# Gated linear attention with two expert layers: chunks prepared two ahead, then three, with other first loads and constant matrices built on the chip

## The chip, the cores and the metric

The kernel runs on one core of a Trainium2 chip. The metric is the time of one launch on the device, in microseconds (us), as the median of several runs. The engines of a core are named as the profile names them: PE (TensorE, matrix products; PEld are its weight loads), DVE (VectorE), ACT (ScalarE), POOL (GpSimd) and SP (SyncE, which here only issues DMAs). Each engine executes its own queue in order; semaphores hold an instruction until what it needs is done.

## The reference

Three layers follow each other. The first is the attention below, over 4 batches, 8 heads, 768 steps and a head width of 48. The second sends each token whose skip score is above zero to the expert with the largest gate logit (8 experts, 384 to 1024 to 384, relu), scales by the gate's probability and adds the token; the third takes the maximum of three products and multiplies by an output matrix.

```python
for t in range(S):
    state = alpha[:, :, t, :, None] * state + np.einsum('bhd,bhe->bhde', k[:, :, t], v[:, :, t])
    y[:, :, t] = np.einsum('bhd,bhde->bhe', q[:, :, t], state)
```

## The kernel before, in words

The sequence of each batch is cut into 6 chunks of 128 steps; 4 batches make 24 chunks, counted n = 0 to 23, and two heads share the 128 partitions, so that a chunk is 4 head pairs wide. The attention takes about the first 135 us; the expert layers, which stay as they are, take the rest. All instructions stand in the order in which the Python code emits them (`manual_schedule`): nothing reorders them afterwards.

For a chunk j, the coefficients, k and q come in one tile `akq` (772.5 KiB: 260.5 of coefficients, 256 each of k and q), of which there are four buffers. `load(j)` fetches all of it, `load_part(j, i)` the coefficients (i = 0), k (1) or q (2), `vload(j)` the values `vt` (200 KiB). All go through SP's one queue. `prep(j)` is made of three parts:

- `suffixes` (L224): a scan on DVE gives the products towards the chunk's end, `sf` (L229); ACT keeps the totals; POOL makes the scaled keys `k` (L232).
- `inverse` (L235): a reciprocal on DVE (L237).
- `prefixes` (L239): a second scan on DVE gives `ap` (L243); ACT does a range test; POOL makes the scaled queries `q` (L247); and `load(j + 4)` is issued on SP into the buffer that j has used up.

The loop over n (L491) then does, in this order: `scores(n+1)` on PE (products `ps`, L272), `trans(n+1)` on PE (transposed keys `pk`, L263), one or two preparations, `mask(n+1)` on DVE in two halves (`sm`, L278; the next scores write into the same two PSUM tiles, so they wait for these), `rows(n-1)` (products `px` on PE, L318, with the constant `rps`; a reduction on DVE, L326), `outs(n)` (products `py` on PE, L305 and L308) and `upd(n)` (products `pu` on PE, L290, to which DVE adds the old state, L293; not for the last chunk of a batch). Which chunks are prepared is `pre` (L492): chunk 2 in turn 0, chunks 3 and 4 in turn 1, and chunk n + 3 in each turn from 2 on. `warm(6)` in turn 1 issues six matmuls on PE whose result nobody reads; `warm(15)` does the same at the start.

`patterns` (L465) is called in turn 3. It fills three small tiles `rst` on POOL and copies them on DVE into `pcs`, which the routing of tokens uses from turn 7 on. In turns 3 to 6, SP also issues 16 writes of a tile of zeros (`zt`) over the DRAM buffer `slots`; the scatters that follow each batch's routing (POOL, L418, `slots<-xr`) go into it and wait for these writes.

Of the kernel before, what the change touches and what calls it, by code (L numbers as in the profile page):

```python
# [9 lines left out]
F32 = mybir.dt.float32  # L10
# [10 lines left out]
NP = H // 2  # L21
# [30 lines left out]
XP = 4  # L52
IX = 6
FIRST = (0, 6, 2)
KEEP = (0, 6)
GT = 512
SOFF = 8192.0 + CAP * NE
LAG = 2
# [23 lines left out]


@with_exitstack
def tile_gla_moe_moe2(ctx, tc, akq, vp, rp, wgt, cst, io, ew, md, out):
    nc = tc.nc
    V, A, G, T, SY = nc.vector, nc.scalar, nc.gpsimd, nc.tensor, nc.sync

# [36 lines left out]
        (eng or V).tensor_tensor(l, src, h.bitcast(F32), ALU.subtract)  # L125

    with tc.manual_schedule():
        cs = const.tile([128, 3 * 128 + NTILE + 8], F32, name="cs")
        rps = const.tile([PR, NP, 105], F32, name="rps")
        ident = cs[:, 0:128]  # L130
        cmask = cs[:, 128:256]
        tokid = cs[:, 384:384 + NTILE]
        rev = cs[:, 384 + NTILE:]
        ltri = const.tile([128, 128], BF16, name="ltri")
        ones = const.tile([128, 128], BF16, name="ones")
        low = const.tile([PR, 1], F32, name="low")
# [48 lines left out]
        zt = w1p.tile([128, XW], F32, name="zt")  # L185
        zero = w1p.tile([128, 1], F32, name="zero")
        ws = [w1p.tile([PR, NP * D + 16], F32, name=f"ws{i}") for i in range(2)]

        def warm(n):
            pw = ps_r.tile([128, 512], F32, name="pr")  # L190
# [16 lines left out]
        def load_part(j, i):  # L207
            raw_[j] = lds[j % LDB]
            z = (slice(0, KW), slice(KW, KW + NP * C), slice(KW + NP * C, AQ))[i]
            SY.dma_start(out=raw_[j][:, z], in_=akq[seq[j]][:, z])  # L210

        def vload(j):
            if j >= nseq:
                return
            b, c = seq[j]
            vt[j] = hp.tile([128, VW], F32, name="vt")
            SY.dma_start(out=vt[j], in_=vp[b, :, c])
# [17 lines left out]
        def inverse(j, sf):  # L235

            V.reciprocal(raw_[j][:, pads], sf[:, pads])  # L237
# [203 lines left out]
            split(h, l, rw[s // 4][:, s % 4 * EW:(s % 4 + 1) * EW], eng)  # L441
            wr[s] = h, l

        for j, i in ((0, 0), (0, 1), (1, 0), (0, 2)):
            load_part(j, i)
        SY.dma_start(out=cs, in_=cst)
        for i in (1, 2):
            load_part(1, i)
        vload(0)
        load(2)  # L450
        SY.dma_start(out=rps, in_=rp)
        vload(1)
        load(3)
        for j in range(2, 5):
            vload(j)
        prep(0)
        for t in ws:
            G.memset(t[:, NP * D:], 0.0)
        G.memset(cnt, 0.0)
        G.memset(zero, 0.0)  # L460
        G.memset(zt, 0.0)
        G.memset(zt[:, DM + 1:], float(1 << 20))
        A.copy(ltri, cs[:, 256:384])
        def patterns():
            for n in (NC, 4, 2):  # L465
                t = w1p.tile([128, NE * (n + 1)], BF16, name=f"rst{n}")
                G.memset(t, 1.0)
                G.memset(t[:, ::n + 1], 0.0)
                V.tensor_scalar(cols[n].bitcast(I32), t.bitcast(I32), 0, None, ALU.bitwise_or)
            V.tensor_copy(cols["rev"], rev)  # L470
# [17 lines left out]
        scores(0)  # L488
        trans(0)
        prep(1)  # L490
        mask(0, 0)  # L491
        mask(0, 1)  # L492
        for n, (b, c) in enumerate(seq):
            pre = [n + 2] if n == 0 else [n + 2, n + 3] if n == 1 else [n + 3]
            pre = [j for j in pre if j < nseq]
            if n + 1 < nseq:
                scores(n + 1)
                trans(n + 1)
            for j in pre:
                prep(j)  # L500
            if n + 1 < nseq:
                mask(n + 1, 0)
                mask(n + 1, 1)
            low_part = rows(n - 1) if n else None
            outs(n)
            upd(n)
            if n > nseq - 4:
                low_part()
            vload(n + 5)
            if n and seq[n - 1][1] == NC - 1:  # L510
                routes.append(route(b - 1, 0, NC))
            step_routes()
            if n < 2:
                warm(KEEP[n])
            if n == 3:
                patterns()
            if n == 10:
                SY.dma_start(out=iota, in_=io)
            if 3 <= n < 7:
                for i in range((n - 3) * NSLOT // 512, (n - 2) * NSLOT // 512):  # L520
                    SY.dma_start(out=slots[i * 128:(i + 1) * 128, :], in_=zt)
            if 7 <= n < 11:
                wpart(n - 7)
# [865 lines left out]
```

## Time and profile before

| | us |
|---|---|
| median of 3 runs | 579.27 |
| lowest and highest | 579.08, 579.62 |
| the profiled execution, whole | 578.67 |
| its span, first to last instruction | 576.9 |
| PE busy in the span | 561.8 (97%) |
| DVE, ACT, POOL busy | 413.9, 299.9, 255.2 |

Times in the rows count from the start of the span. A row of the timeline says when a group of instructions began, how long it lasted, on which engine and line, what it wrote and read, and in square brackets how long the engine had been idle before and what ended that. A matmul of 32-bit data shows as two records. The granted clock of PE is 1.00 throughout.

### The profile page before, as it was taken

To read this page: it belongs to the slowest core of one execution; us is meant where nothing else is said; L and a number is where in the kernel's file an instruction comes from. 1 tells how busy PE (TensorE), PEld (TensorE's weight loads), DVE (VectorE), ACT (ScalarE), POOL (GpSimd) and SP (SyncE) were. 2 spreads that over 40 slices of the span, in tenths; PEclk is the share of its full clock that TensorE was granted. 3 is DMA by queue.
4 is the path that set the end of the run, shared out by engine and by line. 5 is a ranking of instruction groups with operands and counts; after the bars stand their busy time and mean duration, and the time that the engine had idled before them with its cause. 6 is when DMAs were issued, how large, how long until landed. Compare 5 with 4: busy or idle time off the path is not lost. (4 is left out here: it accounts for less than half of the span.)

```text
span 576.9 us, 11055 instructions
## 1 busy us (share of the span) xinstructions
PE 561.8 (97%) x4155; PEld 500.7 (87%) x4155; DVE 413.9 (72%) x727; ACT 299.9 (52%) x641; POOL 255.2 (44%) x202
## 2 busy tenths in 40 slices
PE   7999999999999999999999999999999999999997
PEld 4789888888899999999988888888887899887897
DVE  7988998967577767777679897593767674675710
ACT  3556675654566766666334445454454474445320
POOL 5554598752456555665222122122464400446320
PEclk9999999999999999999999999999999999999999
DMA  8979998925669888885519139515664633556011
GB/s 312 349 236 341 304 326 314 336 116 193 212 217 332 300 302 294 272 306 214 170 27 295 46 121 380 182 55 203 207 241 144 210 119 109 220 177 233 3 55 61
DMA packets 51008, 123.06 MB, mean 213 GB/s; under 512 B 4579, under 2 KB 38865, under 8 KB 47361
## 3 DMA queue, kind: packets, MB, share of 16 engines
q1 hardware_dynamic: 47712, 116.45, 58.4%
q0 software_dynamic: 2560, 4.83, 2.2%
q10 hardware_dynamic: 672, 0.98, 0.6%
q8 instruction: 34, 0.56, 0.4%
q14 instruction: 30, 0.24, 0.1%
HBM read 93.03 MB, written 32.28 MB: 217 GB/s over the span
## 5 line engine op out<-in xcount | busy, mean ns | idle before, releaser
L125 POOL TENSOR_TENSOR wl<-raw,wh 128x768 fp32r<-128x768 f32 x26 | 53.4, 2054 | 32.4 <-ACT wh L124 32.4
L124 ACT CAST wh<-raw 128x768 fp32r<-128x768 f32 x64 | 53.5, 835 | 16.4 <-PE po L696 15.7
L676 PE MATMUL ph<-xh,wh 128*128 128x256 f32 x192 | 56.4, 294 | 0.0
L677 PE MATMUL ph<-xl,wh 128*128 128x256 f32 x192 | 54.5, 284 | 0.1
L678 PE MATMUL ph<-xh,wl 128*128 128x256 f32 x192 | 54.4, 283 | 0.0
L694 PE MATMUL po<-wh,hh 128*128 128x384 f32 x128 | 43.5, 340 | 0.0
L696 PE MATMUL po<-wh,hl 128*128 128x384 f32 x128 | 43.3, 338 | 0.0
L695 PE MATMUL po<-wl,hh 128*128 128x384 f32 x128 | 43.2, 337 | 0.0
L125 DVE TENSOR_TENSOR wl<-raw,wh 128x768 fp32r<-128x768 f32 x38 | 36.2, 953 | 9.2 <-ACT wh L124 9.2
L682 DVE SCALAR_TENSOR_TENSOR hl<-ph,hh 128x256 fp32r<-128x256 f32 x64 | 26.8, 419 | 16.6 <-ACT hh L681 16.5
L232 POOL TENSOR_TENSOR k<-akq,sf 128x512 f32<-128x512 f32 x24 | 28.5, 1187 | 22.0 <-DVE sf L229 16.2
L418 POOL DMA_INDIRECT slots<-xr,si x24 | 24.8, 1034 | 28.0 <-DVE xr L415 11.8
L677 PEld LDWEIGHTS ph<-xl,wh 128*128 128x128 f32 x192 | 36.5, 190 | 0.5 <-DVE xl L125 0.5
L676 PEld LDWEIGHTS ph<-xh,wh 128*128 128x128 f32 x192 | 36.6, 191 | 0.2 <-ACT xh L124 0.2
L678 PEld LDWEIGHTS ph<-xh,wl 128*128 128x128 f32 x192 | 36.4, 190 | 0.0
L272 PE MATMUL ps<-q,k 64*128 64x128 f32 x384 | 30.2, 286 | 6.3 <-POOL q L247 4.4
L272 PEld LDWEIGHTS ps<-q,k 64*128 64x128 f32 x384 | 24.8, 187 | 10.4 <-POOL q L247 5.8
L681 ACT ACTIVATE hh<-ph 128x256 fp32r<-128x256 f32 x64 | 24.5, 383 | 14.3 <-PE ph L678 13.0
L243 DVE TENSOR_TENSOR_SCAN ap<-akq,pcs 128x521 f32<-128x521 f32 x24 | 29.8, 1241 | 2.2
L229 DVE TENSOR_TENSOR_SCAN sf<-akq,pcs 128x520 f32<-128x520 f32 x24 | 29.4, 1226 | 2.4 <-DMA akq<-in_akq_dram 1.5
L278 DVE TENSOR_TENSOR sm<-ps,cs 128x512 f32<-128x512 f32 x48 | 30.3, 674 | 0.9 <-PE ps L272 0.9
L247 POOL TENSOR_TENSOR q<-akq,ap 128x512 f32<-128x512 f32 x24 | 28.4, 1183 | 5.1 <-DVE ap L243 2.6
(655 smaller groups left out, 1720.9 us busy)
## 6 DMA issues: line engine op xcount, KB each, us to landing
raw<-in_ew_dram SPq DMA_DIRECT2D x15, 1536.0 KB, 7.1
akq<-in_akq_dram SPq DMA_DIRECT2D x22, 772.5 KB, 6.0
rm<-in_md_dram SPq DMA_DIRECT2D x12, 768.0 KB, 6.2
mh<-wd SPq DMA_DIRECT2D x7, 1024.0 KB, 5.0
ml<-wd SPq DMA_DIRECT2D x7, 896.0 KB, 6.6
raw<-wd SPq DMA_DIRECT2D x6, 1024.0 KB, 5.1
raw<-wd SPq DMA_DIRECT2D x6, 896.0 KB, 6.5
vt<-in_vp_dram SPq DMA_DIRECT2D x24, 200.0 KB, 6.3
```

Of the source, the lines that this page charges most:

```text
L124: A.copy(h, src)
L125: (eng or V).tensor_tensor(l, src, h.bitcast(F32), ALU.subtract)
L229: V.tensor_tensor_scan(sf[:, KW - 2::-1], al[:, KW - 1:0:-1], eb[:, KW - 1:0:-1], 0.0, ALU.mult, ALU.max)
L243: V.tensor_tensor_scan(ap, al, eb, 0.0, ALU.mult, ALU.max)
L272: T.matmul(ps[i][:, p, :], kh[j][r0:r0 + 64, p, :], qh[j][r0:r0 + 64, p, :], start=True, stop=True)
L278: V.tensor_tensor(t, fr[j][i], cmask[:, None, :].to_broadcast([128, NP, C]), ALU.mult)
L676: T.matmul(ph, wh[:, z], xh_[e][:, k, :], start=(k == 0), stop=False)
L677: T.matmul(ph, wh[:, z], xl_[e][:, k, :], start=False, stop=False)
L678: T.matmul(ph, wl[:, z], xh_[e][:, k, :], start=False, stop=(k == k3 - 1))
L694: T.matmul(po, hh[:, zm], wh, start=(f == 0), stop=False)
L695: T.matmul(po, hh[:, zm], wl, start=False, stop=False)
L696: T.matmul(po, hl[:, zm], wh, start=False, stop=(f == nf1 - 1))
```

## The change

The order of the first loads changes: all three parts of chunk 0 come first, then the coefficients of chunk 1, the constants, the rest of chunk 1, and chunk 2 in three parts. `vload(3)` and `vload(4)` are issued later. The input `rp` (210 KiB) is gone; ACT builds `rps` from the unit matrix and from 36 columns that are now part of `cst`, which is 162 KiB instead of 208 because it no longer carries the matrix for `ltri`. POOL makes `ltri` as a difference of two matrices, in `patterns`.

Turn 0 prepares chunk 2, turn 1 chunk 3, turn 2 chunk 4. From there the lead grows by one in halves: at the end of turns 2, 3 and 4, `first_half` does `suffixes` and `inverse` of chunks 5, 6 and 7, and the following turn does their `prefixes`. From turn 5 on, `prep(n + 3)` is back. The six matmuls of `warm(6)` are gone. The filling of `ws` moves ahead of all loads, that of `cnt` and `zero` into `patterns`, that of `zt` into turn 2.

```diff
-        for j, i in ((0, 0), (0, 1), (1, 0), (0, 2)):
+        for j, i in ((0, 0), (0, 1), (0, 2), (1, 0)):
             load_part(j, i)
         SY.dma_start(out=cs, in_=cst)
+        for j, i in ((1, 1), (1, 2), (2, 0)):
+            load_part(j, i)
+        vload(0)
         for i in (1, 2):
-            load_part(1, i)
-        vload(0)
-        load(2)
-        SY.dma_start(out=rps, in_=rp)
+            load_part(2, i)
         vload(1)
         load(3)
-        for j in range(2, 5):
-            vload(j)
+        vload(2)
         prep(0)
...
         def patterns():
+            G.memset(cnt, 0.0)
+            G.memset(zero, 0.0)
+            G.tensor_tensor(ltri, cmask, ident, ALU.subtract)
             for n in (NC, 4, 2):
...
         prep(1)
+        vload(3)
+        A.copy(rps[:, :, 0:96].rearrange("p a (i d) -> p a i d", i=2),
+               ident.rearrange("p (i d) -> p i d", i=2)[:, None, :, 0:D].to_broadcast([128, NP, 2, D]))
+        A.copy(rps[:, :, 96:], cs[:, 288:].rearrange("p (a e) -> p a e", a=NP))
         mask(0, 0)
         mask(0, 1)
+        ahead = {}
+
+        def first_half(j, n):
+
+            sf = suffixes(j)
+            inverse(j, sf)
+            ahead[n] = j, sf
+
         for n, (b, c) in enumerate(seq):
-            pre = [n + 2] if n == 0 else [n + 2, n + 3] if n == 1 else [n + 3]
-            pre = [j for j in pre if j < nseq]
             if n + 1 < nseq:
                 scores(n + 1)
                 trans(n + 1)
-            for j in pre:
-                prep(j)
+            if n in ahead:
+                prefixes(*ahead.pop(n))
+            if n < RAMP:
+                prep(n + 2)
+            elif n >= RAMP + 2:
+                prep(n + 3)
...
             upd(n)
+            if RAMP <= n + 1 < RAMP + 3:
+                first_half(n + 3, n + 1)
             if n > nseq - 4:
                 low_part()
+            if n == 0:
+                vload(4)
             vload(n + 5)
...
-            if n < 2:
-                warm(KEEP[n])
+            if n == 2:
+                G.memset(zt, 0.0)
+                G.memset(zt[:, DM + 1:], float(1 << 20))
             if n == 3:
                 patterns()
```

On SP, before, the queue starts as follows (`akq_155` is the buffer of chunk 0, `akq_156` of chunk 1, `akq_157` of chunk 2; 128x521 are coefficients, 128x512 k or q, 128x1545 a whole chunk):

```order
L210 DMA akq_155<-in_akq_dram 128x521
L210 DMA akq_155<-in_akq_dram 128x512
L210 DMA akq_156<-in_akq_dram 128x521
L210 DMA akq_155<-in_akq_dram 128x512
L446 DMA cs<-in_cst_dram 128x416
L210 DMA akq_156<-in_akq_dram 128x512 x2
L217 DMA vt<-in_vp_dram 128x400
L205 DMA akq_157<-in_akq_dram 128x1545 [waits DMAHW0_49]
L451 DMA rps<-in_rp_dram 128x420 [waits DMAHW1_49]
```

After, on SP at the same place (`akq_157`, `akq_158` and `akq_159` are now the buffers of chunks 0, 1 and 2):

```order
L213 DMA akq_157<-in_akq_dram 128x521
L213 DMA akq_157<-in_akq_dram 128x512 x2
L213 DMA akq_158<-in_akq_dram 128x521
L449 DMA cs<-in_cst_dram 128x324
L213 DMA akq_158<-in_akq_dram 128x512 x2
L213 DMA akq_159<-in_akq_dram 128x521
L220 DMA vt<-in_vp_dram 128x400 [waits DMAHW0_49]
L213 DMA akq_159<-in_akq_dram 128x512 [waits DMAHW1_49]
```

The queries of chunk 0 are now the third load and the coefficients of chunk 1 the fourth; chunk 2 comes in parts, of which the first is the eighth load.

On DVE, before, from the state update of turn 3 (`pu`, L293) to the masks of chunk 5 (`sm_583`, `sm_585`); the scans `sf` and `ap` here belong to chunk 7:

```order
L293 TENSOR_TENSOR pu<-pu,ws_138 128x192 [waits PE_49]
L469 TENSOR_SCALAR pcs<-rst_543 128x28 [waits DVE_49,Pool_49]
L469 TENSOR_SCALAR pcs<-rst_547 128x20 [waits DVE_49,Pool_49]
L469 TENSOR_SCALAR pcs<-rst_551 128x12 [waits DVE_49,Pool_49]
L470 COPY pcs<-cs 128x8 [waits DVE_49]
L229 SCALAR_TENSOR_TENSOR sf<-akq_158,pcs 128x520 [waits DMAHW3_49,DVE_49]
L237 RECIPROCAL akq_158<-sf 128x4 [waits DVE_49]
L243 SCALAR_TENSOR_TENSOR ap<-akq_158,pcs 128x521 [waits DVE_49]
L278 TENSOR_TENSOR sm_583<-ps_560,cs 128x512 [waits PE_49]
L278 TENSOR_TENSOR sm_585<-ps_561,cs 128x512 [waits PE_49]
```

After, on DVE, from the same update (L296 now) to the same masks (`sm_565`, `sm_567`); the scans here belong to chunk 6:

```order
L296 TENSOR_TENSOR pu<-pu,ws_138 128x192 [waits PE_49]
L232 SCALAR_TENSOR_TENSOR sf<-akq_159,pcs 128x520 [waits DMAHW1_49,DVE_49,Pool_49]
L240 RECIPROCAL akq_159<-sf 128x4 [waits DVE_49]
L468 TENSOR_SCALAR pcs<-rst_531 128x28 [waits Pool_49]
L468 TENSOR_SCALAR pcs<-rst_535 128x20 [waits DVE_49,Pool_49]
L468 TENSOR_SCALAR pcs<-rst_539 128x12 [waits DVE_49,Pool_49]
L469 COPY pcs<-cs 128x8 [waits DVE_49]
L246 SCALAR_TENSOR_TENSOR ap<-akq_159,pcs 128x521 [waits DVE_49]
L281 TENSOR_TENSOR sm_565<-ps_548,cs 128x512 [waits PE_49]
L281 TENSOR_TENSOR sm_567<-ps_549,cs 128x512 [waits PE_49]
```

The copies of `patterns` now stand between the two scans of one chunk, and the chunk that is prepared here is one lower.

On POOL, before, around `patterns` (`k_487` and `q_494` belong to chunk 6, `k_573` to chunk 7):

```order
L232 TENSOR_TENSOR k_487<-akq_157,sf 128x512 [waits DMAHW1_49,DVE_49,PE_49]
L247 TENSOR_TENSOR q_494<-akq_157,ap 128x512 [waits DVE_49,PE_49]
L467 MEMSET rst_543 128x56
L468 MEMSET rst_543 128x8 [waits Pool_49]
L467 MEMSET rst_547 128x40
L468 MEMSET rst_547 128x8 [waits Pool_49]
L467 MEMSET rst_551 128x24
L468 MEMSET rst_551 128x8 [waits Pool_49]
L232 TENSOR_TENSOR k_573<-akq_158,sf 128x512 [waits DMAHW3_49,DVE_49]
```

After, on POOL, at the same place (`k_523` and `q_562` belong to chunk 6):

```order
L235 TENSOR_TENSOR k_523<-akq_159,sf 128x512 [waits DMAHW1_49,DVE_49,PE_49]
L461 MEMSET cnt 128x8
L462 MEMSET zero 128x1
L463 TENSOR_TENSOR ltri<-cs 128x128
L466 MEMSET rst_531 128x56
L467 MEMSET rst_531 128x8 [waits Pool_49]
L466 MEMSET rst_535 128x40
L467 MEMSET rst_535 128x8 [waits Pool_49]
L466 MEMSET rst_539 128x24
L467 MEMSET rst_539 128x8 [waits Pool_49]
L250 TENSOR_TENSOR q_562<-akq_159,ap 128x512 [waits DVE_49,PE_49]
```

The tiles `rst` are now filled behind the keys of chunk 6 and behind three added instructions, and ahead of that chunk's queries.

## Rows read from the trace of the kernel before

**Rows 1.** Busy time by stretch: length, then us and instructions per engine, clock, DMA.

```profile
core 0: us, PE busy (x) PEld busy (x) DVE busy (x) ACT busy (x) POOL busy (x), PEclk, DMA share, GB/s
35.00:40.00 5.00, 4.59 (x65) 4.02 (x62) 4.90 (x9) 3.27 (x11) 3.17 (x3) 1.00 0.87 263
45.00:50.00 5.00, 5.00 (x78) 4.55 (x77) 4.55 (x14) 3.70 (x13) 1.78 (x2) 1.00 1.05 343
200.00:577.00 377.00, 371.86 (x1985) 329.89 (x1983) 253.70 (x383) 181.36 (x324) 137.60 (x90) 1.00 0.52 179
```

**Rows 2.** Waits of PE: to 130 us, then from there: total, times, longest.

```profile
PE ps L272 <- POOL q L247: 4.4, 5, 1.2
...
PE pt L664 <- DMA xs<-slots: 1.2, 1, 1.2
```

**Rows 3.** Timeline of the first 16 us.

```profile
1.34 5.99 PE L192 MATMUL pr<-wu,ones 128*128 128x512 bf16 x15 [1.34 <-DVE wu L168]
...
6.20 1.24 DVE L229 TENSOR_TENSOR_SCAN sf<-akq,pcs 128x520 f32<-128x520 f32 x1
...
7.13 1.17 POOL L247 TENSOR_TENSOR q<-akq,ap 128x512 f32<-128x512 f32 x1 [1.15 <-DMA akq<-in_akq_dram]
...
11.34 1.16 PE L272 MATMUL ps<-q,k 64*128 64x128 f32 x16 [1.24 <-POOL q L247]
...
15.50 1.16 PE L272 MATMUL ps<-q,k 64*128 64x128 f32 x16 [0.93 <-POOL q L247]
```

**Rows 4.** Timeline from 20 to 28 us: six idle matmuls, masks, two scores.

```profile
20.55 1.47 PE L192 MATMUL pr<-wu,ones 128*128 128x512 bf16 x6
...
20.67 1.26 DVE L278 TENSOR_TENSOR sm<-ps,cs 128x512 f32<-128x512 f32 x2
...
21.95 1.19 PE L272 MATMUL ps<-q,k 64*128 64x128 f32 x16
...
27.02 1.16 PE L272 MATMUL ps<-q,k 64*128 64x128 f32 x16
```

**Rows 5.** Timeline of DVE from 27 to 51 us, and the scores behind it.

```profile
27.41 1.23 DVE L229 TENSOR_TENSOR_SCAN sf<-akq,pcs 128x520 f32<-128x520 f32 x1
...
30.12 1.26 DVE L278 TENSOR_TENSOR sm<-ps,cs 128x512 f32<-128x512 f32 x2
...
32.19 0.37 DVE L293 TENSOR_TENSOR pu<-pu,ws 128x192 f32<-128x192 f32 x1 [0.70 <-PE pu L290]
...
32.47 0.75 DVE L469 TENSOR_SCALAR pcs<-rst 128x28 int32<-128x28 int32 x3
...
33.70 1.24 DVE L229 TENSOR_TENSOR_SCAN sf<-akq,pcs 128x520 f32<-128x520 f32 x1
...
50.72 1.26 DVE L278 TENSOR_TENSOR sm<-ps,cs 128x512 f32<-128x512 f32 x2
...
51.53 1.66 PE L272 MATMUL ps<-q,k 64*128 64x128 f32 x16
```

**Rows 6.** Timeline of POOL: a small fill, scaled queries, the first `rst`.

```profile
8.33 0.10 POOL L459 MEMSET cnt<- 128x8 bf16 x1
...
30.35 1.18 POOL L247 TENSOR_TENSOR q<-akq,ap 128x512 f32<-128x512 f32 x1 [0.40 <-DVE ap L243]
...
31.47 0.14 POOL L467 MEMSET rst<- 128x56 bf16 x1
```

**Rows 7.** Timeline from 63 to 78 us: the first scatter, chunk 12, two waits.

```profile
63.45 1.14 POOL L418 DMA_INDIRECT slots<-xr,si  x1 [7.06 <-DMA raw<-in_ew_dram]
...
64.84 1.24 DVE L243 TENSOR_TENSOR_SCAN ap<-akq,pcs 128x521 f32<-128x521 f32 x1
...
67.02 1.19 POOL L247 TENSOR_TENSOR q<-akq,ap 128x512 f32<-128x512 f32 x1
...
68.26 1.16 PE L272 MATMUL ps<-q,k 64*128 64x128 f32 x16 [0.47 <-POOL q L247]
...
77.85 1.16 PE L272 MATMUL ps<-q,k 64*128 64x128 f32 x16 [0.69 <-POOL q L247]
```

More of the change, by code (lines that the diff above doesn't have):

```diff
@@ L54 @@
 FIRST = (0, 6, 2)
-KEEP = (0, 6)
+RAMP = 3
 GT = 512
@@ L84, in tile_gla_moe_moe2 @@
 @with_exitstack
-def tile_gla_moe_moe2(ctx, tc, akq, vp, rp, wgt, cst, io, ew, md, out):
+def tile_gla_moe_moe2(ctx, tc, akq, vp, wgt, cst, io, ew, md, out):
     nc = tc.nc
@@ L127, in tile_gla_moe_moe2 @@
     with tc.manual_schedule():
-        cs = const.tile([128, 3 * 128 + NTILE + 8], F32, name="cs")
+        cs = const.tile([128, 2 * 128 + NTILE + 8 + NP * 9], F32, name="cs")
         rps = const.tile([PR, NP, 105], F32, name="rps")
@@ L131, in tile_gla_moe_moe2 @@
         cmask = cs[:, 128:256]
-        tokid = cs[:, 384:384 + NTILE]
-        rev = cs[:, 384 + NTILE:]
+        tokid = cs[:, 256:256 + NTILE]
+        rev = cs[:, 256 + NTILE:288]
         ltri = const.tile([128, 128], BF16, name="ltri")
@@ L187, in tile_gla_moe_moe2 @@
         ws = [w1p.tile([PR, NP * D + 16], F32, name=f"ws{i}") for i in range(2)]
+        for t in ws:
+            G.memset(t[:, NP * D:], 0.0)
         def warm(n):
@@ L442, in wsplit @@
             wr[s] = h, l
-        for j, i in ((0, 0), (0, 1), (1, 0), (0, 2)):
+        for j, i in ((0, 0), (0, 1), (0, 2), (1, 0)):
             load_part(j, i)
         SY.dma_start(out=cs, in_=cst)
+        for j, i in ((1, 1), (1, 2), (2, 0)):
+            load_part(j, i)
+        vload(0)
         for i in (1, 2):
-            load_part(1, i)
-        vload(0)
-        load(2)
-        SY.dma_start(out=rps, in_=rp)
+            load_part(2, i)
         vload(1)
         load(3)
-        for j in range(2, 5):
-            vload(j)
+        vload(2)
         prep(0)
[L457 to L463, printed above, removed]
         def patterns():
+            G.memset(cnt, 0.0)
+            G.memset(zero, 0.0)
+            G.tensor_tensor(ltri, cmask, ident, ALU.subtract)
             for n in (NC, 4, 2):
@@ L1348 @@
     vv[..., :H * D] = v.reshape(B, H, NC, 128, D).transpose(0, 3, 2, 1, 4).reshape(B, 128, NC, H * D)
-    rp = np.zeros((2, 64, NP, 105), f32)
-    for i in range(2):
-        for d in range(D):
-            rp[i, d, :, i * D + d] = 1.0
     wg = np.concatenate([inputs["moe_w_gate"], inputs["moe_w_skip"][:, None]], axis=1)
-    rp[:, :D, :, 96:] = wg.reshape(NP, 2, D, 9).transpose(1, 2, 0, 3)
-    rp = rp.reshape(128, NP, 105)[:PR]
-    cst = np.zeros((128, 3 * 128 + NTILE + 8), f32)
+    wr = np.zeros((2, 64, NP, 9), f32)
+    wr[:, :D] = wg.reshape(NP, 2, D, 9).transpose(1, 2, 0, 3)
     i = np.arange(128)
-    cst[:, 0:128] = i[:, None] == i[None, :]
-    cst[:, 128:256] = i[:, None] <= i[None, :]
-    cst[:, 256:384] = i[:, None] < i[None, :]
-    cst[:, 384:384 + NTILE] = i[:, None] + 128 * np.arange(NTILE)[None, :]
-    cst[:, 384 + NTILE:] = np.arange(8, 0, -1)[None, :]
+    cst = np.concatenate([i[:, None] == i[None, :], i[:, None] <= i[None, :],
+                          i[:, None] + 128 * np.arange(NTILE)[None, :], np.broadcast_to(np.arange(8, 0, -1), (128, 8)),
+                          wr.reshape(128, NP * 9)], axis=1).astype(f32)
     ew = np.empty((NE, 128, FF // 128, EW), f32)
@@ L1372 @@
     ins = {"akq": akq, "vp": vv,
-           "rp": rp, "wgt": wg, "cst": cst,
+           "wgt": wg, "cst": cst,
            "io": np.broadcast_to(np.arange(512, dtype=f32), (128, 512)), "ew": ew.reshape(NE, 128, -1), "md": md}
```

## The prediction

> **What bounds the kernel now.** I read the busy time by stretch first, then PE's waits, then the timeline of the first 80 us. From 200 us to the end PE is busy 371.86 of 377 us [rows 1], and the only wait of PE on a transfer behind the attention is 1.2 us for `xs<-slots` [rows 2], which itself follows the scatters and so moves with them. So whatever PE is early or late when the attention ends stays to the end. Inside the attention PE's losses are at the start: 4.4 us in five waits for scaled queries [rows 2], of which 1.24 and 0.93 stand ahead of the scores of chunks 1 and 2 [rows 3]. A turn of pure PE work is 5.07 us (27.02 less 21.95 [rows 4]). But PE is not alone at the limit. Between 32.19 and 50.72 us [rows 5] DVE goes from the state update of turn 3 to the masks of chunk 8 almost without a hole: 4.90 and 4.55 us of two stretches of 5 [rows 1], the second made of 14 short instructions with their gaps. The scores of chunk 9 follow at 51.53, half a mask behind [rows 5]. There DVE, not PE, sets the pace, and that decides this case.
>
> **First loads.** Loads land in the order of issue. Before, the third load (777 KiB up to its end) has landed by 6.20, where its scan starts, and the fourth (1033 KiB) ends a wait of POOL at 7.13 [rows 3], so it lands at 7.08. After, the queries of chunk 0 are third, and `q` of chunk 0 waits only for its scan, ending 6.21: POOL starts 0.9 earlier. The coefficients of chunk 1 are fourth: their scan starts at 7.1 instead of 6.20, 0.9 later. A preparation costs DVE 2.71 us, from the start of a scan to the mask behind it (30.12 less 27.41 [rows 5]). So chunk 1 is through at 9.8, its queries at 9.85 + 1.18 = 11.05 (1.18 is a `q` [rows 6]), its scores at 11.1 instead of 11.34. The masks of chunk 0 take 1.3 [rows 4], the preparation of chunk 2 starts at 11.1 and ends at 13.85, its queries at 15.05: scores of chunk 2 at 15.1 instead of 15.50. I take 0.4 early; with loads that land no earlier it is 0, with all the gain of chunk 0's queries 0.9.
>
> **Two ahead and no filler.** Before, 6.45 us pass from the scores of chunk 2 to those of chunk 3 (15.50 to 21.95 [rows 3, 4]): PE's 5.07 and 1.38 more, in which DVE does two preparations ahead of the masks (20.67) and PE runs the six idle matmuls, 1.47 us [rows 4]. After, one preparation stands there: DVE is done with chunk 3 and the masks of chunk 2 by 15.1 + 2.7 + 1.3 = 19.1, ahead of PE's 15.1 + 5.07 = 20.2. PE gains 0.4 + 1.4 = 1.8 and keeps it while DVE is ahead, to the state update of turn 3: 32.19 - 1.8 = 30.4.
>
> **The preparation that is owed.** At that update DVE had prepared chunks 0 to 6 before; after, 0 to 5. By the masks of chunk 8 both have prepared all up to chunk 10, so the same packed row of work, 18.53 us, now holds one preparation more, 2.71 us, and starts 1.8 earlier: 0.9 late.
>
> **A new wait in turn 3.** The three copies of `rst` followed the state update directly before and waited for nothing (32.47, right behind 32.19 [rows 5]). After, they stand on DVE behind the scan of chunk 6, and on POOL the filling of `rst` is queued behind the keys of chunk 6, which need that scan. From the scan's end: keys 1.18, then `cnt` and `zero` (0.1 each at most [rows 6], partly overlapped, 0.1 together), `ltri`, and the first `rst` (two fills of about 0.14 [rows 6]). `ltri` has no row: by columns it is a quarter of a 128x512 product, 0.3; if columns didn't count, 1.18. I take 0.3, since its row differs from it in width alone. That is 1.95 with the hand-over; DVE is free 0.2 after the scan (the reciprocal). So DVE waits about 1.7 us, 1.3 to 2.6 by the bounds, and behind it on DVE are `ap` of chunk 6, the masks of chunk 5, and so the queries and scores of chunk 6.
>
> **What comes back.** DVE reaches the masks of chunk 8 at 30.4 + 18.53 + 2.71 + 1.7 = 53.3 instead of 50.72: 2.6 late, and the scores of chunk 9 with it. Before, POOL then stands behind a scatter that begins at 63.45 only, when the zeros have landed, and it works off a backlog: `q` of chunk 12 starts at 67.02, though its scan ended at 66.08, 0.94 earlier; PE waits for POOL 0.47 and 0.69 ahead of chunks 12 and 14 [rows 7]. A DVE that is 2.6 late hides 0.94 of that on POOL (1.66 left) and 1.16 on PE (1.44 left); the later one counts, 1.7 at chunk 14.
>
> **The rest.** The fills of `ws` go to an idle POOL at the start, that of `zt` ahead of queries which wait for their scan anyway; without that cover they cost 0.1 each [rows 6] and a few tenths. ACT's two copies for `rps` (busy 3.27 of 5 us where it is fullest here [rows 1]) are first read some 5 us later. `vload(3)` now queues on SP behind the load of chunk 5, which waits for the queries of chunk 1 (11.05); it is read by PE from about 22 on. 256 KiB fewer are loaded; no wait behind the first 16 us hangs on that, since DVE is late and not early.
>
> **Sum.** 1.8 gained, 2.71 + 1.7 owed, 0.94 hidden: 1.67 us longer, 580.3 for the profiled execution of 578.67. The median of the runs is 579.27, 0.6 above that execution; by the same difference I forecast 581.0.
>
> **Rivals.**
> 1. The gain stays (faster): if DVE had slack between 32.19 and 50.72, the masks of chunk 5 would be ready when PE ends turn 4, and 1.8 would remain: 577.5. It decides at one place: whether PE, free at about 35.0, finds the masks of chunk 5 done. For it: DVE's 4.55 of 5 us, if those gaps are real slack. Against: 2.6 us of slack are needed, and the two stretches leave 0.55.
> 2. The wait doesn't bind: POOL fills `rst` early enough, or the hidden part is larger. Without the 1.7, DVE is 0.9 late, 1.3 if the loads bring nothing, and 0.94 is hidden on POOL: 0 to 0.4 longer, 579.3 to 579.7. For it: the fills themselves are short. Against: the order of the program puts them behind the keys of chunk 6, and nothing else on POOL could let them pass.
> 3. The zeros decide: loads of chunks 10 and 11 now leave behind the late queries of chunks 6 and 7, into a stretch where the DMA engines already run at 0.87 to 1.05 [rows 1]. One whole chunk more, 772.5 KiB, at the 343 GB/s of that stretch is 2.3 us. If the first scatter (63.45 [rows 7]) moves by more than the 1.7, it sets the time: up to 2.3 longer, 581.6.
> 4. PE slows: the granted clock is 1.00 in all rows [rows 1], yet the first 15 matmuls of 512 columns take 0.40 each and the six of turn 1 0.245 (5.99/15, 1.47/6 [rows 3, 4]), so the first run near the level of 1.2 GHz, the later ones at 2.4. The idle 1.24 ahead of chunk 1 brought no slow scores (1.16 before and after it [rows 3]). After, PE idles about 2.4 us ahead of chunk 6 (35.0 to 37.4, when its queries are done). If it then ran a turn at half rate, 5 us become 10; DVE, by then 1.7 ahead of its need, hides part: some 3 us more, 584. The Trainium skill (TensorE: Matmul & The Clock Gate, Part 1) says that the array is throttled by default, that activity releases it and idling brings the throttle back; it speaks for the filler that is removed. By it the time would be that of this rival, if the hole is long enough; the trace has no hole of this length, so it is open.
>
> **Chances and range.** Forecast 0.50, rival 1 0.12, rival 2 0.25, rival 3 0.08, rival 4 0.05. The forecast's own range comes from the wait (1.3 to 2.6) and the start (0 to 0.9 instead of 0.4): 580.2 to 582.0. Down to 579.0 it takes in rival 2, up to 582.2 rival 3; left out are rivals 1 and 4, 0.17. A measurement of this kernel tells about 0.2%, 1.2 us, from no change: slower is rivals 3 and 4 and 0.45 of the forecast, 0.58; faster is rival 1, 0.12; within it 0.30.
>
> **What would show it.** Right: scores of chunk 3 near 20.2; the copies of `rst` start about 1.7 us behind the reciprocal of chunk 6, released by POOL; scores of chunk 6 near 37.4, of chunk 9 near 54.1, of chunk 14 near 79.5. Wrong: copies of `rst` without idle time before them (rival 2); masks of chunk 5 ended by 35 (rival 1); the first scatter past 65.2 with its wait on a transfer and POOL packed behind it (rival 3); scores with twice the usual 1.16 (rival 4). If chunk 14 is late as forecast but the end is not, a stage behind the attention has slack that I read as none.

## The result, and the profile after

| | before | after |
|---|---|---|
| median, us | 579.51 (7 runs) | 582.54 (7 runs) |
| lowest and highest | 579.08, 580.43 | 580.89, 583.42 |
| the profiled execution, whole | 578.67 | 581.82 |
| its span | 576.9 | 580.0 |

The ratio is 1.0051, with a 95% interval of 1.0041 to 1.006: the change costs 3.0 us. It is slower, as forecast, but the time lies above the range (582.2), and the 3.0 us are 1.8 times the forecast 1.7.

Busy time by stretch after, in the columns of [rows 1]:

```profile
35.00:40.00 5.00, 3.11 (x26) 2.92 (x26) 4.93 (x9) 1.87 (x7) 2.53 (x3) 0.79 0.67 190
40.00:45.00 5.00, 4.95 (x55) 4.07 (x55) 4.76 (x7) 2.36 (x7) 3.33 (x3) 0.87 1.03 277
45.00:50.00 5.00, 5.00 (x70) 4.72 (x69) 4.56 (x14) 3.80 (x13) 2.37 (x2) 1.00 0.98 341
200.00:580.00 380.00, 374.10 (x1995) 331.15 (x1993) 255.41 (x384) 182.30 (x326) 139.11 (x91) 1.00 0.53 179
```

PE is idle for 1.9 of the 5 us from 35 on, where [rows 1] had 0.4, and the granted clock is 0.79 and 0.87 in the first two stretches, between its two levels of 1.2 and 2.4 GHz. DVE is as full as before. The timeline of the first 80 us after shows where this comes from:

```profile
6.47 1.24 DVE L232 TENSOR_TENSOR_SCAN sf<-akq,pcs 128x520 f32<-128x520 f32 x1 [0.19 <-DMA akq<-in_akq_dram]
...
14.39 1.16 PE L275 MATMUL ps<-q,k 64*128 64x128 f32 x16 [0.66 <-POOL q L250]
19.44 1.16 PE L275 MATMUL ps<-q,k 64*128 64x128 f32 x16
...
29.66 0.37 DVE L296 TENSOR_TENSOR pu<-pu,ws 128x192 f32<-128x192 f32 x1 [0.70 <-PE pu L293]
...
31.20 0.18 DVE L240 RECIPROCAL akq<-sf 128x4 f32<-128x4 f32 x1
31.30 1.18 POOL L235 TENSOR_TENSOR k<-akq,sf 128x512 f32<-128x512 f32 x1 [2.20 <-PE ps L275]
...
32.52 0.45 POOL L463 TENSOR_TENSOR ltri<-cs 128x128 bf16<-128x128 f32 x1
...
33.27 0.76 DVE L468 TENSOR_SCALAR pcs<-rst 128x28 int32<-128x28 int32 x3 [1.89 <-POOL rst L466]
...
36.89 1.23 PE L275 MATMUL ps<-q,k 64*128 64x128 f32 x16 [2.62 <-POOL q L250]
...
38.96 1.87 PE L321 MATMUL px<-rps,yt 128*128 128x105 f32 x8
...
53.30 1.66 PE L275 MATMUL ps<-q,k 64*128 64x128 f32 x16 [0.25 <-DVE sm L281]
...
65.07 1.15 POOL L421 DMA_INDIRECT slots<-xr,si  x1 [6.92 <-DMA vt<-in_vp_dram]
...
69.89 1.16 PE L275 MATMUL ps<-q,k 64*128 64x128 f32 x16 [0.33 <-POOL q L250]
...
79.49 1.16 PE L275 MATMUL ps<-q,k 64*128 64x128 f32 x16 [0.70 <-POOL q L250]
```

The scores of chunk 3 start at 19.44 instead of 21.95 [rows 4]. DVE waits 1.89 us for POOL's `rst`; behind it PE stands 2.62 us ahead of the scores of chunk 6, and then `px` takes 1.87 us where it takes 1.04 a turn later. The scores of chunk 9 are 1.77 late (53.30 for 51.53 [rows 5]), those of chunk 14 1.64 (79.49 for 77.85 [rows 7]). The first scatter is late by 1.62 (65.07 for 63.45 [rows 7]). From the first matmuls behind the attention to the last of all, after:

```profile
154.41 0.41 PE L682 MATMUL pt<-cs,xs 128*128 128x128 f32 x2 [1.28 <-DMA xs<-slots]
...
575.05 0.34 PE L1115 MATMUL pt<-mh,hb1l 128*128 128x384 f32 x1
```

and before, at the same two places:

```profile
152.77 0.41 PE L664 MATMUL pt<-cs,xs 128*128 128x128 f32 x2 [1.18 <-DMA xs<-slots]
...
572.86 0.34 PE L1097 MATMUL pt<-mh,hb1l 128*128 128x384 f32 x1
```

PE is 1.64 late at the first and 2.19 at the last; the span is 3.1 longer. So of the 3.15 us between the two profiled executions 1.64 come from the attention, 0.55 arise in code that the diff doesn't touch, and 1.0 behind the last matmul. On its way the lateness falls to 1.25 near 280 us and rises from 390 us on.

### The profile page after: what moved, and what is told of

Its sections match the earlier page's. It is cut to its first block, busy times and chain, and to the rows that moved or that the text cites. A ratio compares the mean times of both kernels' runs of the same rounds, so it can differ in the third digit from the quotient of the medians.

```text
span 580.0 us, 11044 instructions
## 1 busy us (share of the span) xinstructions
PE 562.9 (97%) x4149; PEld 501.3 (86%) x4149; DVE 414.0 (71%) x727; ACT 300.6 (52%) x642; POOL 256.0 (44%) x203
## 4 chain that ended last, share of the span: by engine, by line
PE 64%; DVE 7%; DMA 3%; issue 2%; ACT 2%; POOL 1%; DVEq 0%; POOLq 0%; ACTq 0%
PE ph L694 4%; PE ph L695 4%; PE ph L696 4%; PE po L714 3%; PE po L713 3%; PE po L712 3%; PE po L1043 3%; PE po L1045 3%; PE po L1044 3%; PE ph L1043 3%; PE ph L1045 3%; PE ph L1044 3%; DMA wd<-cl 2%; PE ph L882 2%; PE ph L881 2%
```

## The experiments

Each kernel is compared with the kernel before on the same chip; "late" and "early" are PE's times against the profiled execution of the kernel before. The kernels ran on several chips, on which the kernel before takes between 579.4 and 587.4 us; the last section says where two of them lose the time. One profiled execution differs from the next by some tenths of a us from the start on: in the thirteen with the new loads and the new ramp the scores of chunk 3 are 1.8 to 2.8 early.

**`rst` filled early.** POOL's fills move to the end of turn 1; the definition of `fills` is left out here.

```diff
+            if n == 1:
+                fills()        # cnt, zero, ltri, rst on POOL
             if n == 3:
-                patterns()     # fills and copies
+                patterns()     # the copies on DVE alone
```

> The changed kernel, but POOL fills `cnt`, `zero`, `ltri` and the three `rst` at the end of turn 1 and not in turn 3; DVE copies `rst` at the same place as in the changed kernel. The wait theory: the 1.89 us of idle DVE in front of the first copy is gone, so is the 2.62 us hole of PE ahead of the scores of chunk 6 and the half-rate clock behind it; DVE is then about 0 to 0.4 late at the masks of chunk 8, and the attention ends where it did before. If nothing else costs, 579.3 to 580.0. The rival that some 1.4 us of the loss lie outside the attention (another layout in memory, other loads): the attention as just said, but the end at 580.7 to 581.3. The rival that the owed preparation alone is the cost, and the wait falls into slack: 582.0 to 583.

Measured: 580.68 against 579.44, ratio 1.0018 (1.0009 to 1.0027). Timeline, then a stretch, of this kernel:

```profile
31.74 0.18 DVE L240 RECIPROCAL akq<-sf 128x4 f32<-128x4 f32 x1
31.84 0.60 DVE L473 TENSOR_SCALAR pcs<-rst 128x28 int32<-128x28 int32 x3
...
41.64 1.66 PE L275 MATMUL ps<-q,k 64*128 64x128 f32 x16 [1.61 <-DVE sm L281]
...
63.13 1.14 POOL L421 DMA_INDIRECT slots<-xr,si  x1 [5.65 <-DMA akq<-in_akq_dram]
...
77.56 1.16 PE L275 MATMUL ps<-q,k 64*128 64x128 f32 x16
```

```profile
40.00:45.00 5.00, 3.34 (x28) 3.03 (x27) 4.77 (x7) 2.12 (x7) 3.04 (x3) 0.86 1.07 287
```

The wait is gone. PE is still 1.43 late at chunk 9 (1.77 with the wait), but the first scatter now starts at 63.13 and not at 65.07, behind it chunk 14 is 0.3 early, and from 90 us on PE is within 0.1 of the kernel before. So the wait was worth 1.6 us of the attention, and DVE's lateness was not slack. The time is not that of the wait theory alone (up to 580.0) but nearest that of the rival with a part of the loss outside the attention. The hole has only moved, to 1.61 us ahead of chunk 7, where DVE pays for the owed preparation, and the clock falls there.

**Unread matmuls in the hole.**

```diff
+            if n == 4:
+                warm(6)
```

> The changed kernel with six matmuls on PE that nobody reads behind turn 4, in the hole ahead of the scores of chunk 6 (1.5 of its 2.6 us); the wait of DVE stays. The clock theory: the granted clock stays 1.0 from 37.8 to 41.3 us, and the end comes earlier by up to 1.7 us, which is half of the 3.4 us at half rate: 580.8 to 581.9. The rival that DVE sets the pace of chunks 7 to 9 and hides the slow matmuls: the same time as the changed kernel, 582.2 to 582.9, with or without the clock's fall.

Measured: 581.22 against 579.44, ratio 1.0032 (1.0021 to 1.0044), where the change has 1.0051: by the ratios 1.1 us shorter. The same kernel was run again beside the changed one:

> The changed kernel, unaltered, as the measure for the other three on the same chip: 2 to 3 us longer than the kernel before, with a spread of 2 us or more and a granted clock of 0.993 to 0.999.

> The changed kernel with six unread matmuls behind turn 4, in the hole ahead of the scores of chunk 6. The clock theory: 0.8 to 1.5 us shorter than the changed kernel, with a narrower spread and the clock nearer to 1.0. The rival that the clock's fall is hidden by DVE, as the one profiled execution reads: within 0.4 us of it.

Measured on this chip: the kernel before 580.75, the changed kernel 584.04 (ratio 1.0067, 1.0049 to 1.0085), with the six matmuls 582.35 (1.0039, 1.0025 to 1.0052): 1.7 us shorter. Two stretches of the changed kernel here:

```profile
35.00:40.00 5.00, 3.06 (x22) 2.84 (x23) 4.93 (x9) 1.18 (x6) 2.46 (x3) 0.72 0.64 186
40.00:45.00 5.00, 4.95 (x58) 4.19 (x57) 4.77 (x7) 2.99 (x8) 3.39 (x3) 0.94 1.03 264
```

and with the matmuls:

```profile
35.00:40.00 5.00, 3.80 (x45) 3.08 (x45) 4.93 (x9) 2.37 (x8) 2.71 (x3) 1.00 0.61 162
40.00:45.00 5.00, 3.41 (x44) 2.71 (x40) 4.74 (x8) 1.76 (x5) 3.26 (x4) 1.00 1.04 266
```

The clock stays at 1.00, and DVE's busy time is the same: in these two executions it sets the pace either way, and the last matmul starts at 575.86 and 575.75. So the medians show a gain of 1.7 us that the profiled pair (582.97 and 582.35, the first the lowest of its six runs) shows only in part. The mean granted clock is on record for every run. It is on average 0.9979 in the kernel before, 0.9962 in the changed kernel and 0.9979 with the matmuls; 0.0017 of 581 us is 1.0 us of full speed, which the matmuls give back. A second sign of what the clock costs is the kernel before itself: of its 20 runs on this chip, the 8 with a mean clock of 0.999 or more have a median of 579.84, the 12 below that 581.28.

**The new ramp alone**, with the loads, constants and early fills of the kernel before (the change's hunks in the loop, without `vload(4)` and `zt`).

```diff
-            pre = [n + 2] if n == 0 else [n + 2, n + 3] if n == 1 else [n + 3]
...
+            if n in ahead:
+                prefixes(*ahead.pop(n))
+            if n < RAMP:
+                prep(n + 2)
+            elif n >= RAMP + 2:
+                prep(n + 3)
...
+            if RAMP <= n + 1 < RAMP + 3:
+                first_half(n + 3, n + 1)
...
-                warm(KEEP[n])
```

> The kernel before with the new loop alone: two ahead, then three, no idle matmuls; loads, constants and fills on POOL as before (so `rst` is still filled on POOL behind the keys of chunk 6, but without `cnt`, `zero` and `ltri` in front). By the wait theory DVE waits some 1.3 us ahead of the first copy of `rst`, start gain 1.4 to 1.8, one preparation owed: 579.9 to 580.8. If the new loads and constants carry the loss, 579.2 to 579.7. If the ramp carries all of it, 582 to 583.

Measured: 580.48 against 579.44, ratio 1.0025 (1.0013 to 1.0038), as the wait theory has it. The wait is there too, shorter by what `cnt`, `zero` and `ltri` take:

```profile
34.28 0.76 DVE L469 TENSOR_SCALAR pcs<-rst 128x28 int32<-128x28 int32 x3 [1.40 <-POOL rst L467]
```

PE is 1.84 late behind the attention and 1.72 at the end: here nothing is lost in the later stages.

**The new loads and constants alone**, with the loop and the six matmuls of the kernel before. Against the changed kernel (the lines that go, and the fills that return to the start, are left out):

```diff
+            pre = [n + 2] if n == 0 else [n + 2, n + 3] if n == 1 else [n + 3]
...
+            for j in pre:
+                prep(j)
...
+            if n < 2:
+                warm(KEEP[n])
```

> The changed kernel with the loop of before: its new loads, the matrices built on the chip, but two preparations in turn 1 and the six idle matmuls, and POOL's `cnt`, `zero` and `zt` filled at the start. By the wait theory 578.9 to 579.6, with the scores of chunk 3 up to 0.9 earlier than 21.95. If another layout in memory or the constants cost the 1.4 us that lie outside the attention: 580.5 to 581.3, with the attention on time and the lateness behind 280 us.

Measured: 579.56 against 579.44, ratio 1.000 (0.999 to 1.0009). PE is 0.9 early from chunk 2 to 60 us, 0.19 early behind the first scatter, and 0.33 late at the last matmul. The loads gain what the prediction hoped from them, the first scatter takes most of it, and a drift behind 390 us the rest.

**One size.** The tile of the constants in SBUF back to 416 columns, of which 324 are used; run beside the changed kernel on one chip.

```diff
-        cs = const.tile([128, 2 * 128 + NTILE + 8 + NP * 9], F32, name="cs")
+        cs = const.tile([128, 416], F32, name="cs")[:, 0:324]
```

> The changed kernel, unaltered, beside the others of this call: 582.0 to 583.0. By the clock theory its runs spread wide (2 us or more) because the matmuls at half rate fall in different places from run to run; a second profile then has a hole of PE of over 1.6 us ahead of the scores of chunk 6 and a stretch at about half clock behind it, and more of it stays to the end than the 2.2 us by which PE was late in the first profile. The rival that the spread comes from the last store alone: PE is late by 2.0 to 2.3 us at the last matmul again.

> The changed kernel with one size changed: the tile of the constants takes 416 columns of each partition as before, of which 324 are loaded and used, so that all later tiles stand where they stood before. If the place of the tiles in SBUF is what makes PE 0.35 us faster from 135 to 290 us and 0.85 us slower from 390 to 530 us than in the kernel before (the kernel with the new ramp alone showed neither), PE keeps its lateness of the attention flat to the end, 1.6 us, and the time is 0.5 shorter: 581.7 to 582.3. If it is the layout in DRAM or another thing, the two slopes stay: 582.2 to 583.

Measured: the kernel before 587.42, the changed kernel 589.5 (1.0032, 1.0014 to 1.005), padded 589.3 (1.0036, 1.0018 to 1.0054). In the traces the slopes are nearly gone: between 160 us and the last matmul the changed kernel's lateness goes from 8.91 over 8.54 to 9.56, that of the padded one from 10.22 to 10.48. The times differ less than they are uncertain, and how wide the changed kernel's runs spread says nothing here, where those of the kernel before go from 584.54 to 589.0. A second pair, each with the six matmuls in the hole, was run beside the two kernels of the experiment above:

> The same six matmuls, and the tile of the constants padded to 416 columns. What is left is then the wait and the owed preparation: by the sum of the prediction 1.6 us longer than the kernel before (1.3 to 2.0), 0.3 to 0.6 shorter than with the six matmuls alone. If the placement doesn't count in the median: the same as with the six matmuls alone.

Measured: 582.26, ratio 1.0025 (1.0013 to 1.0037), beside 1.0039 without the padding. First and last matmul behind the attention, padded:

```profile
155.20 0.41 PE L684 MATMUL pt<-cs,xs 128*128 128x128 f32 x2 [1.35 <-DMA xs<-slots]
...
575.30 0.34 PE L1117 MATMUL pt<-mh,hb1l 128*128 128x384 f32 x1
```

and not padded:

```profile
154.91 0.41 PE L684 MATMUL pt<-cs,xs 128*128 128x128 f32 x2 [1.21 <-DMA xs<-slots]
...
575.75 0.34 PE L1117 MATMUL pt<-mh,hb1l 128*128 128x384 f32 x1
```

From the one row to the other the padded kernel takes 420.10 us, the kernel before 420.09, the unpadded one 420.84. Over all profiled executions it is 420.33 to 420.84 in the ten with the tile of 324 columns and 419.82 to 420.33 in the ten with 416. The place of the tiles costs PE some 0.6 us; the medians of this pair (582.35 and 582.26) differ by 0.1, less than they are uncertain.

**A longer wait**, on top of the padded kernel.

```diff
+            for _ in range(4):
-            G.tensor_tensor(ltri, cmask, ident, ALU.subtract)
+                G.tensor_tensor(ltri, cmask, ident, ALU.subtract)
...
-                warm(6)
+                warm(11)
```

> As the padded kernel with unread matmuls (eleven, so that the longer hole is filled as well), but POOL makes `ltri` four times over, at 0.4 us each, ahead of the first `rst`: DVE's wait in turn 3 grows from 1.9 to about 3.1 us. By the theory that this wait counts in full, since nothing is left to hide it, 1.1 to 1.3 us longer than the padded kernel. If POOL's backlog behind the first scatter still hides some: 0 to 0.7 longer.

Measured: 583.69, ratio 1.0064 (1.0047 to 1.0081), 1.4 us longer than the padded kernel. The waits of DVE:

```profile
DVE pcs L469 <- POOL rst L467: 3.5, 1, 3.5
```

The wait is 1.6 longer and the copies start 1.26 later; behind the attention PE is 3.53 late instead of 2.36. What DVE loses here reaches the end of the attention almost whole.

**Zeros a turn earlier**, in four kernels.

```diff
-            if 3 <= n < 7:
-                for i in range((n - 3) * NSLOT // 512, (n - 2) * NSLOT // 512):
+            if 2 <= n < 6:
+                for i in range((n - 2) * NSLOT // 512, (n - 1) * NSLOT // 512):
```

In the kernel before, on two chips:

> The kernel before with one edit: the 16 writes of zeros in turns 2 to 5 and not 3 to 6. The gate theory: in the kernel before, too, the first scatter waits for the zeros until 63.4 us and POOL's backlog behind it costs PE 0.47 and 0.69 ahead of chunks 12 and 14; with the zeros landed by 59 both waits go, 0.9 to 1.2 us faster than the kernel before. That is then also the part of DVE's lateness that any kernel with late zeros hides. The rival that the zeros delay the loads of chunks 6 to 8: no faster.

> The kernel before with the zeros in turns 2 to 5, a second time, beside the changed kernel with the same edit: again 1.2 to 2.8 us faster than the kernel before. By the theory of the wait and the owed preparation, the changed kernel with this edit is 1.8 us or more slower than this one, since nothing is left that hides DVE's lateness.

Measured: 577.64 against 580.41, ratio 0.9952 (0.9938 to 0.9966), and 583.73 against 585.32, 0.9975 (0.9964 to 0.9985). This one edit beats both kernels. Timeline, then waits of PE from 60 to 95 us, on the first chip:

```profile
59.88 1.14 POOL L418 DMA_INDIRECT slots<-xr,si  x1 [3.64 <-DMA raw<-in_ew_dram]
```

```profile
PE ps L272 <- DVE sm L278: 0.9, 3, 0.4
```

PE no longer waits for POOL there, and is 1.2 early behind the attention, 0.1 of it from the start; on the second chip it is 0.55 early, 0.3 late at the start. So the landing of the zeros, the gate in front of the first scatter, costs PE 0.9 to 1.1 us in the kernel before. The medians gain more, 2.8 and 1.6 us: the mean clock of the runs is also higher, by 0.0010 and 0.0012, which is 0.6 and 0.7 us; what is left on the first chip stays unexplained.

The gate sets the end of the attention in the changed kernel too. In all twelve profiled executions of altered kernels that write the zeros in turns 3 to 6, PE is late at chunk 14 by what the first scatter is late, to 0.04 us, however late PE was at chunk 9: 1.64 for 1.62 in the changed kernel, -0.19 for -0.19 with the new loads alone, 1.82 for 1.81 with the new ramp alone. On the chip on which it ran beside the kernel with the six matmuls the changed kernel has

```profile
65.92 1.14 POOL L421 DMA_INDIRECT slots<-xr,si  x1 [7.72 <-DMA akq<-in_akq_dram]
...
80.34 1.16 PE L275 MATMUL ps<-q,k 64*128 64x128 f32 x16 [0.70 <-POOL q L250]
```

which is 2.47 and 2.49 late, after 1.82 at chunk 9: there the scatter adds time. With the new loads:

> The new loads and constants with the ramp of before, and the 16 writes of zeros a turn earlier, in turns 2 to 5. If the landing of the zeros is what gates the first scatter at 63.2 us and with it POOL, the scatter starts at 58 to 60, the scores of chunk 12 no longer wait for `q`, and PE keeps the 0.9 us that it is early up to 60 us: 578.4 to 579.1, faster than the kernel before. If another thing gates it, or the zeros delay the loads of chunks 6 to 8: 579.4 to 580.5.

Measured: 583.9 against 587.42, ratio 0.9944 (0.9926 to 0.9963); PE is 1.08 early at 60 us and 1.91 at 120. In the changed kernel, beside the second of the two runs above:

> The changed kernel with the zeros in turns 2 to 5; the wait of DVE in turn 3 and the ramp stay. If the landing of the zeros ends the attention in the changed kernel, the first scatter starts by 61.5 and not at 65, and PE is 0.3 to 0.9 late at 100 us and not 1.6: 0.7 to 1.3 us shorter than the changed kernel. If DVE alone ends it, PE stays 1.6 to 1.8 late there and the time is that of the changed kernel within 0.3, some 3 us longer than the kernel before.

Measured: 587.7, ratio 1.0042 (1.003 to 1.0054), 4.0 us slower than the kernel before with the same edit, and 2.4 slower than the kernel before as it was. The changed kernel itself has ratios from 1.0032 to 1.0067 on other chips, so a gain from the zeros is not shown here. The first scatter starts at 62.2, but PE is 1.35 late at 100 us, not 0.3 to 0.9: it was 2.2 late at chunk 9 here. The kernel before with this edit is 0.55 early at 100 us on this chip, so without the gate the lateness that the change leaves is 1.9 us, DVE's own. The rest of the 4.0 lies behind the attention or in the clock, whose mean over the runs is 0.991 for 0.997.

**The ramp, without its wait and its hole.** Six matmuls behind turn 5 and `rst` filled early (first run); then also earlier zeros and padding, with the ramp of before and with the new one.

```diff
+            if n == 1:
+                fills()
...
+            if n == 5:
+                warm(6)
```

> POOL's fills in turn 1, as in the run that moved them, and six matmuls that nobody reads behind turn 5, in the 1.61 us hole of PE ahead of the scores of chunk 7 that this run still had and behind which the granted clock fell. The clock theory: the clock stays 1.0, PE is not 1.5 late at 45 us but about 0.8, which DVE sets; the attention ends at most 0.1 us off the kernel before, and the time is 579.9 to 580.4 with a narrow spread. The rival that the clock's fall is hidden behind the first scatter: the same as without these matmuls, 580.4 to 581.0.

Measured: 586.6 against 587.42, ratio 0.9992 (0.9974 to 1.001), beside 1.0032 for the changed kernel on this chip. With the wait gone and the hole filled the loss is gone, although the tile of the constants still has 324 columns. The clock stays at 1.00:

```profile
40.00:45.00 5.00, 4.74 (x50) 3.74 (x50) 4.77 (x9) 2.23 (x7) 2.82 (x4) 1.00 1.07 267
```

PE is 0.75 early at chunk 8, where it was 1.48 late without these six matmuls; 0.6 of the difference stems from the start. Behind the attention it is 0.5 late, not 0.1 as expected, and so is the first scatter (63.90 for 63.45).

> The new loads and constants with the ramp of before, zeros a turn earlier, and the tile of the constants padded to 416 columns. By the placement theory the drift behind the attention (0.3 to 0.65 us longer in the end with 324 columns) goes: PE's lead over the kernel before at 140 us, about 1.9, is its lead at the last matmul to within 0.2; 1.7 to 2.2 us faster than the kernel before. If padding is not the cause: 1.2 to 1.6 faster, and the lead shrinks between 390 and 530 us.

> The changed kernel with its ramp, but `rst` filled in turn 1, six unread matmuls behind turn 5, zeros a turn earlier, padded constants. By the theory of the owed preparation DVE is still 0.3 us early to 0.3 late at the masks of chunk 8, where the ramp of before with the same loads is 1.1 early; so 0.6 to 1.2 us faster than the kernel before, and 0.8 to 1.4 slower than the same edits with the ramp of before. If the ramp itself costs nothing once the wait and the clock's fall are gone: equal to the ramp of before, 1.7 to 2.2 faster.

Measured against 580.41: 577.86 with the ramp of before (0.9958, 0.9943 to 0.9972), 578.1 with the new one (0.9954, 0.994 to 0.9969): no difference in the medians, where 0.8 to 1.4 us were expected: they speak for the rival that the ramp costs nothing once the wait and the clock's fall are gone. In the traces there is a difference. The scores of chunks 9 and 17, with the ramp of before:

```profile
51.02 1.66 PE L275 MATMUL ps<-q,k 64*128 64x128 f32 x16
...
92.34 1.66 PE L275 MATMUL ps<-q,k 64*128 64x128 f32 x16 [0.36 <-DVE sm L281]
```

and with the new one:

```profile
51.96 1.66 PE L275 MATMUL ps<-q,k 64*128 64x128 f32 x16 [0.25 <-DVE sm L281]
...
93.28 1.66 PE L275 MATMUL ps<-q,k 64*128 64x128 f32 x16 [0.36 <-DVE sm L281]
```

The new ramp is 1.3 earlier at chunk 3 and 0.94 later from chunk 9 on: the owed preparation costs 2.3 us there, and 0.9 net of the gain at the start. The intervals are too wide to show that.

**The debt put off**, with early `rst`, early zeros and padding.

```diff
-RAMP = 3
+RAMP = 12
```

> The changed kernel with `rst` filled in turn 1, zeros a turn earlier and padded constants, and two ahead kept up to chunk 13: the third preparation is caught up in turns 11 to 14 and not 2 to 5. If the cost of the changed ramp is where the owed preparation falls (between 30 and 50 us, where DVE has no slack), PE keeps the 2.0 to 2.5 us that it is early at chunk 3 up to 58 us without a hole of over 1 us, and the end is 1.5 to 2.5 faster than the kernel before. The rival that two ahead leaves POOL no lead over the scatters: PE waits 1 us or more for `q` in each of the turns 9 to 13, and the time is 1 to 5 us longer than the kernel before.

Measured: 582.58 against 580.41, ratio 1.0036 (1.0022 to 1.0049). The lead is 2.0 at 30 us and, after a hole of 1.3 ahead of chunk 6, still 1.0 to 1.6 from chunk 7 to chunk 10 (55.6 us); then the scatters come:

```profile
58.55 1.15 POOL L421 DMA_INDIRECT slots<-xr,si  x1 [3.44 <-DMA vt<-in_vp_dram]
...
63.37 1.50 PE L275 MATMUL ps<-q,k 64*128 64x128 f32 x16 [2.63 <-POOL q L250]
```

With two ahead, `q` of the next chunk stands on POOL behind two scatters; PE goes from 1.5 early to 1.3 late there and is 3.1 late at 90 us; the granted clock falls behind this hole as well, to 0.90 and 0.75 in the two stretches of 5 us from 60 on. The third chunk of lead is needed by the first scatter.

## Why the prediction was wrong in size

**The start: right, but too small.** The scores of chunk 3 gained 2.51, not 1.8. The coefficients of chunk 1 were there at 6.47, not 7.1, so the scores of chunk 2 gained 1.11 and not 0.4; the other 1.4, from the second preparation and the idle matmuls, is as forecast. Part of the difference is chance: the thirteen executions have 1.8 to 2.8.

**The debt and the new wait: right.** From the state update of turn 3 (29.66, 2.53 early) to the scores of chunk 9 (1.77 late) DVE lost 4.30 us; the sum had 2.71 + 1.7 = 4.41. The wait is 1.89 (forecast 1.7, `ltri` 0.45 and not 0.3), which leaves 2.4 for the preparation. Three experiments bear it out: without the wait the attention ends 1.6 earlier, with a wait 1.6 longer 1.2 later, and with the ramp alone the wait is still there.

**What comes back: wrong.** The step "a DVE that is 2.6 late hides 0.94 of that on POOL" took the first scatter to stay at 63.45. It moved to 65.07, because the zeros queue on SP behind loads which wait for queries that are now late. The last four writes, before and after:

```profile
51.49 2.03 SPq L521 DMA_DIRECT2D slots<-zt  x4
```

```profile
51.92 2.79 SPq L539 DMA_DIRECT2D slots<-zt  x4
```

The last of them was issued at 54.2 instead of 53.1. The third was issued 1.0 later and landed at 63.8 instead of 62.1, so 0.7 of the delay arose on the way; why is not shown. Only 0.13 came back. This is the mechanism of rival 3, which had 0.08: at 1.62 us it is just short of the point from which it would add time, and on two other chips the scatter of the changed kernel is 2.1 and 2.5 late against the one profile of the kernel before and does add time, 0.3 and 0.7 us. The two errors, 0.7 at the start and 0.8 here, cancel: the attention is 1.64 late, forecast 1.67. That is luck, and a sum that comes out right with two wrong terms is not yet a right account: the gate is worth 0.9 to 1.1 us in the kernel before, and no term or rival saw that moving it alone would make the kernel faster.

**"Whatever PE is early or late when the attention ends stays to the end": this step failed.** The sum ends there, and 1.5 us of the profiled difference lie behind it (1.4 of that of the medians). Part is a size that I costed at nothing: `cs` is 92 columns smaller, so every later tile stands elsewhere in SBUF, and PE's time behind the attention grows by 0.55; padding the tile brings it back, in all six padded kernels to within 0.3 of the kernel before. The remaining 1.0 lies behind the last matmul, where the last store is made; the four profiled executions of kernels that keep all of the old layout have 3.5 to 3.8 us from there to the end of the span, the three of the changed kernel 4.6 to 5.7, the seven others with the small tile 4.0 to 5.1. Five of the padded kernels have 3.9 to 4.2, but the sixth has 5.3, so that this belongs to the layout is not shown.

**Rival 4 got too small a chance.** It had 0.05 and 584. Its mechanism occurred: idle 2.62 us, then a clock of 0.79 and 0.87 in two stretches, in sum 1.7 us of full speed lost (0.21 and 0.13 of 5 us). The Trainium skill (TensorE: Matmul & The Clock Gate, Part 1) says that idling brings the throttle back, and the trace agrees here. In the profiled execution DVE, which sets the pace of chunks 7 to 9 anyway, hides it; in the medians, filling the hole with unread matmuls gives back 1.1 and 1.7 us. The sign that was named for this rival, scores of twice the usual 1.16, did not come: those of chunk 6 took 1.23, and `px` behind them 1.87 for 1.04. The idle matmuls that the change removed had no work that the profile shows, and I priced only their time.

**What stays open.** How the 1.4 us outside the attention divide between the place of the tiles, the last store and the clock in a typical run. The attention's 1.64, the place's 0.55 and the 1.1 to 1.7 of the filled hole come to more than the 3.0 measured; the first two are read in single executions and the third in medians, and no profiled execution shows where a typical run loses it, though its mean clock does (1.0 us). The kernel without the wait and with the hole filled has 0.9992 with the small tile, so neither the place nor the last store is shown to cost a typical run anything.

**The chances.** Slower had 0.58, and of the five signs named for it the copies held by POOL, chunk 6 (36.89 for 37.4) and chunk 14 (79.49 for 79.5) came as named, chunks 3 and 9 each 0.8 earlier (19.44 for 20.2, 53.30 for 54.1). The range failed, by 0.3 us, because it stopped at rival 3 and left rival 4 out. Its own bounds for the wait and the start add up to 580.1 to 582.3, not to 580.2 to 582.0, and 0.2 of the 0.3 is that the kernel before measured 579.51 and not 579.27.

## What to carry to other kernels

A preparation saved at the start is only put off; before taking it, find the stretch in which it will be done and ask whether the engine that does it has holes there, and whether the lead it gave is needed by then. When a step moves behind another engine's queue, follow the queue of each engine it touches, and when everything gets later, follow the transfers that gate the next stage too: here moving that gate alone made the kernel before 1.6 to 2.8 us faster, which no part of the change did. A tile whose size changes moves all tiles behind it, so keep its size when you compare, and fill a hole of an engine whose clock can fall before you judge what the hole costs.

## What was not expected of the hardware

The same matmuls took 420.33 to 420.84 us instead of 419.82 to 420.33 between two fixed places when the tiles in SBUF stood 368 bytes per partition lower (92 columns of 4 bytes); why was not tried.

On two of the chips every kernel profiled stands still near 125 us. In the changed kernel on the first of them, DVE waits 6.25 us for something that the profile calls only `remote`, and PE stands still for 3.3 us in the same place; on the other chips the same update follows without it:

```profile
131.44 0.37 DVE L296 TENSOR_TENSOR pu<-pu,ws 128x192 f32<-128x192 f32 x1 [6.25 <-remote]
```
